# Pinning the first batch ahead of everything else in a linear-attention and Fourier-mixing kernel

## The chip, the cores and the metric

One core of one Trainium2 chip. The metric is device time in microseconds (us); a kernel's figure is the median of its runs, with the lowest and highest beside it. Engines are named as in the profile: PE is TensorE (matmuls), DVE is VectorE, ACT is ScalarE, POOL is GpSimd, SP is SyncE, which issues the input loads and the stores. "Landed" means that a transfer's data are in place, and "the cast" always means ScalarE's conversion of batch 2's first queries.

## The reference, cut to what matters

Batches are counted from 0 to 3. Each has 8 heads of 768 steps; the kernel takes heads in pairs, four to a batch.

```python
for t in range(S):                       # linear attention with decay, q, k, v: (4, 8, 768, 64)
    state = gamma * state + outer(k[:, :, t], v[:, :, t])
    y[:, :, t] = scale * (q[:, :, t] @ state)
x = y.transpose(0, 2, 1, 3).reshape(4, 768, 512)
mixed = real(fft(fft(x, axis=1), axis=2))            # mixing
u = x + mixed
un = (u - mean(u)) / sqrt(var(u) + 1e-6)
out = u + relu(un @ w_ch1) @ w_ch2                   # w_ch1 (512, 2048), w_ch2 (2048, 512)
```

## The kernel before, as far as the argument touches it

The loads of one head pair are three transfers, q, k and v of 384 KB each. `after` ties them to a weight transfer:

```python
def load_unit(b, i, after=None):
    def run():
        for name, src in srcs.items():
            t = inp.tile([P, 2, NCH, D], f32, tag="in32", name=f"{name}32")
            dma = nc.sync.dma_start(t, ...)                       # issued by SP
            if after is not None:
                tc.add_manual_dep(dma.ins, w_dma[after].ins.name, ...)   # "loads in turn"
# ... cut ...
def w1_unit(g):                                                   # w2_unit is alike; eight in all
    def run():
        w_dma.append(nc.gpsimd.dma_start(w116[...], moe_w_ch1[...]))     # issued by GpSimd, 512 KB
# ... cut ...
streams.append(([load_unit(1, i, 6) for i in range(4)], -0.1, 0.0))     # batch 1 waits for the 7th
```

Queries are cast to 16 bits on GpSimd for batches 0 and 1, on ScalarE for batches 2 and 3:

```python
def cast_unit(b, i):
    ...
        if b < NPE:                                    # NPE = 2
            ... nc.gpsimd.tensor_scalar(out=q16, in0=q32...)
        else:
            q16 = qzs[i % 2]
            for h2 in range(2):
                dst = q16[:, h2, :, D * h2:D * h2 + D]
                nc.scalar.copy(dst, q32[:, h2])        # "q16z<-q" on ACT
```

The first batch is a list of units (`un`) whose order is pinned on every engine. The rest is a set of streams: each has a start and an end on a common scale (1.0 is a batch), the units are sorted by it, and this gives each engine's order:

```python
un += [q0_unit(3), w1_unit(0), t0_unit(3, 0), te_unit(3, 0), filler(2)] + y(2)    # fourth pair
un += [yx_unit(2), ..., k0_unit(3), filler(2), ..., v0_unit(3), w1_unit(1), csn_unit(0), ...]
# ... cut ...
streams += [(majors, b, b + 1.0),                      # the two big matmuls, h (psh) and ch (psc)
            (mix_units(b, [3, 4, 5]), b + (0.12 if b == 0 else 0.02), b + 0.3)]
...
    ts = [0.04 + 0.57 * sum(n[:j]) / sum(n) for j in range(7)]    # attention of the next batch
    streams.append((mix_units(b + 1, [0, 1, 2]), b + ts[-1] + 0.09, b + ts[-1] + 0.24))
```

`filler(n)` is n matmuls on zeros that only keep TensorE busy.

Of the kernel before, what the change touches and what calls it, by code (L numbers as in the profile page):

```python
# [11 lines left out]
AF = mybir.ActivationFunctionType  # L12
ALU = mybir.AluOpType
# [5 lines left out]
P = 128  # L19
# [3 lines left out]
NCH = S // P  # L23
# [11 lines left out]
def kernel(  # L35
# [50 lines left out]
    sgn = const.tile([P, 1], f32, tag="sgn")  # L86


    tails = {}
    mark = [0]  # L90

    def pin(engines=None):
        ins = tc.nc.cur_bb.bb.instructions
        for n in range(mark[0], len(ins)):
            x = ins[n]
            e = str(x.engine)
            if engines is not None and not any(g in e for g in engines):
                continue
            if e in tails:
                tc.add_manual_dep(x, tails[e],  # L100
                                  mybir.DependencyInfo(mybir.DependencyClass.NoSync,
                                                       mybir.DependencyReason.DATA),
                                  reason="pinned order")
            tails[e] = x.name
        mark[0] = len(ins)


    ht16 = hp_.tile([P, NFB, 384], f16, tag="ht16")
# [3 lines left out]
    def filler(n):  # L112
        def run():
            for _ in range(n):
                nc.tensor.matmul(wps, wz[:, 0:P], wz, start=True, stop=True)  # L115
        return run
# [36 lines left out]
    icoln = const.tile([P, 5], f32, tag="icoln")  # L153
    hpi = const.tile([P, 1], f32, tag="hpi")

    nc.gpsimd.memset(wz, 0.0)  # L156
    nc.gpsimd.iota(icol_i[:, 0:3], pattern=[[P, 3]], base=0, channel_multiplier=1)
    nc.gpsimd.iota(icol_i[:, 3:5], pattern=[[P, 2]], base=1, channel_multiplier=1)
    nc.gpsimd.iota(icol_i[:, 5:6], pattern=[[0, 1]], base=127, channel_multiplier=-1)
    nc.gpsimd.iota(kf_i, pattern=[[1, KN]], base=0, channel_multiplier=0)  # L160
    filler(8)()
    for h in range(H):
        nc.vector.memset(lgrow[:, h:h + 1], float(lng[h]))
    nc.vector.memset(maskf, 1.0)
    nc.vector.memset(gkrow, 0.0)
    for h in range(H):
        nc.vector.memset(gkrow[D * (h % 2):D * (h % 2) + D, h // 2, 1:NCH - 1],
                         float(gam[h] ** P))
    nc.vector.tensor_copy(icol[:, 0:6], icol_i[:, 0:6])
    nc.vector.tensor_scalar(out=gexp[:, 0], in0=lgrow, scalar1=icol[:, 3:4],  # L170
                            scalar2=float(math.log(0.125)), op0=ALU.mult, op1=ALU.add)
    nc.vector.tensor_scalar(out=gexp[:, 1], in0=lgrow, scalar1=icol[:, 5:6], scalar2=None,
                            op0=ALU.mult)
    nc.scalar.activation(gexp, gexp, AF.Exp, bias=0.0, scale=1.0)
    make_identity(nc, ident16)
    nc.gpsimd.affine_select(out=maskf, in_=maskf, compare_op=ALU.is_ge, fill=0.0, base=0,
                            pattern=[[1, P]], channel_multiplier=-1)
# [4 lines left out]
    nc.vector.tensor_scalar(out=icoln[:, 3:5], in0=icol[:, 3:5], scalar1=float(1.0 / DM),  # L182
                            scalar2=None, op0=ALU.mult)
    nc.vector.tensor_copy(kf, kf_i)

    def gk_unit(hp):
        def run():
# [50 lines left out]

    def csn_unit(c):
        def run():  # L240
            nc.gpsimd.tensor_scalar(out=csn[:, c, :].rearrange("p (i t) -> p t i", t=2),
                                    in0=csp[:, :, c, 0:192], scalar1=1.0, scalar2=1.0,
                                    op0=ALU.mult, op1=ALU.mult)
        return run

    def td_dve(c):
        return trig_dve(3 + c, DM, 257, icol[:, 3 + c:4 + c], icoln[:, 3 + c:4 + c])
# [672 lines left out]
    def first_units():  # L920
        def a(i):
            un = [am_unit(i, 0), am_unit(i, 1)]
            return un

        def e(i, *hh):
            return [ae_unit(i, half, h2) for half, h2 in hh]

        def y(i):
            return [yi_unit(i, 0), yi_unit(i, 1)]

        def x(i):
            return [x0_unit(i, 0), x0_unit(i, 1)]

        std = ((0, 0), (0, 1), (1, 0), (1, 1))
        heads = ((0, 0), (1, 0), (0, 1), (1, 1))
        o = PAIR_ORDER
        un = [ts_dve(0), gk_unit(o[0]), gk_unit(o[1]), t_act(0, 0), t_act(0, 1), q0_unit(0),
              t0_unit(0, 0), filler(6), ts_dve(1), te_unit(0, 0), t_act(0, 2), ts_dve(2),
              t_act(1, 0), k0_unit(0), t0_unit(0, 1), filler(2), te_unit(0, 1), v0_unit(0),
              t_act(1, 1), t_act(1, 2)]  # L940
        un += a(0) + [filler(1), kv0_unit(0)] + e(0, *std) + [sc_unit(0)]
        un += [q0_unit(1), t0_unit(1, 0), t_act(2, 0), te_unit(1, 0), filler(2)] + y(0)
        un += [td_dve(0), t_act(2, 1), k0_unit(1), t0_unit(1, 1), te_unit(1, 1), yx_unit(0),
               filler(1)] + x(0) + [v0_unit(1), half_ids]
        un += a(1) + [kv0_unit(1)] + e(1, *std) + [sc_unit(1), t_act(2, 2), gk_unit(o[2])]
        un += [q0_unit(2), t0_unit(2, 0), te_unit(2, 0), filler(2)] + y(1)
        un += [td_dve(1), parity_consts, t_act(3, 0), t_act(3, 1), k0_unit(2), t0_unit(2, 1),
               te_unit(2, 1), yx_unit(1), filler(1)] + x(1) + [v0_unit(2)]
        un += a(2) + [kv0_unit(2)] + e(2, *std) + [sc_unit(2), t_act(3, 2), gk_unit(o[3])]
        un += [q0_unit(3), w1_unit(0), t0_unit(3, 0), te_unit(3, 0), filler(2)] + y(2)  # L950
        un += [yx_unit(2), fold_s(0, 0, 258, 0, 1), g0_unit(0, (0,)), k0_unit(3), filler(2),
               x0_unit(2, 0), t0_unit(3, 1), te_unit(3, 1), x0_unit(2, 1), filler(3),
               v0_unit(3), w1_unit(1), csn_unit(0), csn_unit(1), csn_unit(2)]
        un += [w1_unit(g) for g in range(2, 4)] + [w2_unit(g) for g in range(4)]
        un += a(3) + e(3, (0, 0), (1, 0)) + [kv0_unit(3), filler(3), sc_unit(3),
               t_act(4, 0), t_act(4, 1)]
        un += e(3, (0, 1), (1, 1))
        un += [yx_unit(3), yi_unit(3, 0), x0_unit(3, 0), filler(2), yi_unit(3, 1), x0_unit(3, 1),
               g0_unit(0, (1,))]
        un += [fold_s(0, 0, 130, 1, 2), fold_d(0, 0, (0,)), s1_unit(0, 0, 0), t_act(4, 2),  # L960
               fold_s(0, 130, 258, 1, 2), fold_d(0, 0, (1,)), fold_d(0, 1, (0,)), px_unit(0),
               xmean_unit(0), fold_d(0, 1, (1,)), s1_unit(0, 1, 0), s1_unit(0, 0, 1),
               s1_unit(0, 1, 1), px_unit(1), filler(1), g0_unit(0, (2,)), mean_unit(0)]
        un += [s2_unit(0, 0), s2_unit(0, 1), norm_unit(0, 0), gr_unit(0), gr_unit(1),
               px_unit(2), filler(4), unT_unit(0, 0), xmean_unit(1), mean_unit(1),
               norm_unit(0, 1), s2_unit(0, 2), xmean_unit(2), mean_unit(2), norm_unit(0, 2),
               gr_unit(2), gr_unit(3), edge_zeros, x_edges(1)]
        return un

    def mix_units(b, kbs):  # L970
        return [s2_unit(b, kb) for kb in kbs] + [unT_unit(b, kb) for kb in kbs]

    def emit(streams):
        ev = []
        for si, (units, t0, t1) in enumerate(streams):
            for i, u in enumerate(units):
                ev.append((t0 + (t1 - t0) * (i + 1.0) / len(units), si, i, u))
        ev.sort(key=lambda e: e[:3])
        for e in ev:
            e[3]()  # L980
            if e[0] < 1.0:
                pin(None if e[0] < 0.05 else ["Pool", "GpSimd"])

    pin()
    for u in first_units():
        u()
        pin()
    first.close()
    ps_pm = pool("ps_pm", 3, space=PSUM)
    late_consts()  # L990
    streams = []
    for b in range(B):
# [6 lines left out]
        else:  # L999
# [3 lines left out]
        majors += [h_unit(b, 1, fb) for fb in range(NFB)]  # L1003
        majors.append(rstd_unit(b, 1))
        majors += [ch_unit(b, 1, rb3, part) for rb3 in range(3) for part in range(4)]
        streams += [(majors, b, b + 1.0),
                    (mix_units(b, [3, 4, 5]), b + (0.12 if b == 0 else 0.02), b + 0.3)]
        if b + 1 < B:
            steps = attn_steps(b + 1)
            if b == 0:  # L1010
                streams.append(([load_unit(1, i, 6) for i in range(4)], -0.1, 0.0))
                streams.append(([qt_zeros], 0.1, 0.15))
                streams.append(([pad_unit], 0.9, 0.95))
                ts = (0.27, 0.31, 0.34, 0.42, 0.51, 0.60, 0.67, 0.74)
            else:
                streams.append(([load_unit(b + 1, i) for i in range(4)], b - 0.3, b + 0.15))
                n = [len(u) for u in steps]
                ts = [0.04 + 0.57 * sum(n[:j]) / sum(n) for j in range(7)]
                ts.insert(1, ts[1])
            streams.append((steps[0], b + ts[0], b + ts[1]))  # L1020
            streams += [(u, b + ts[j + 2], b + ts[j + 3]) for j, u in enumerate(steps[1:])]
            streams.append(([s1_unit(b + 1, 0, 1), s1_unit(b + 1, 1, 1)], b + ts[-1] + 0.04,
                            b + ts[-1] + 0.06))
            streams.append((mix_units(b + 1, [0, 1, 2]), b + ts[-1] + 0.09, b + ts[-1] + 0.24))
    emit(streams)


# [28 lines left out]
```

## Time and profile before

| kernel before | |
|---|---|
| median of 3 runs | 265.85 us (265.15 to 265.86) |
| span of the profiled run (a run of 264.69 us) | 263.0 us |
| PE, DVE, ACT, POOL busy | 92%, 70%, 44%, 29% |
| first h matmul, start | 39.48 us |
| loads of batch 1 released (seventh weight landed) | 42.75 us |
| the cast, start | 67.50 us |

Busy shares are averages over stages. The row of slices (a fortieth of the span each, busy share in tenths) shows the stages, and the chain, the waits and the timeline say what ended each wait. The lines that my prediction rested on are shown inside it. One row of the same page I passed over, the granted clock of TensorE in tenths of full speed:

```profile
PEclk9898899999999999999999999999999999999999
```

Three slices of the first five hold an 8: part of the time in them was granted at half speed (a clock of 0.50 for 3.41 us from 11.04 us and again from 24.69).

### The profile page before, as it was taken

How to read it: one execution, taken by the hardware profiler on the slowest of the kernel's cores; microseconds unless marked ns; L12 is line 12 of the kernel's file. 1: busy time of each engine (PE TensorE's matmuls, PEld its weight loads, DVE VectorE, ACT ScalarE, POOL GpSimd, SP SyncE). 2: the span in 40 equal slices, each digit the busy share in tenths (PEclk: the TensorE clock that was granted, in tenths of full speed). 3: DMA queues.
4: the chain of work that ended last, by engine and by line, in shares of the span. 5: the costliest groups of instructions: out<-in, count | busy, mean ns of one | idle time of the engine just before them, and what ended most of it. 6: DMA issues, size and time to landing. Idle time of an engine off the chain costs nothing.

```text
span 263.0 us, 5235 instructions
## 1 busy us (share of the span) xinstructions
PE 242.4 (92%) x2020; PEld 148.1 (56%) x2020; DVE 184.2 (70%) x446; ACT 115.9 (44%) x238; POOL 75.1 (29%) x132
## 2 busy tenths in 40 slices
PE   7497799979999998999999999999999999999993
PEld 2265468946675554766566545656567456445541
DVE  7889974959799876798885654997886737523421
ACT  3886469573574344564336422541245305402300
POOL 5776600398233042543201411410001303100000
PEclk9898899999999999999999999999999999999999
DMA  8999999999999899979974042264110231211012
GB/s 174 265 246 137 199 193 220 256 228 267 213 242 194 111 241 189 219 148 175 241 192 91 0 100 82 50 122 110 42 40 0 42 122 37 45 55 64 0 42 80
DMA packets 97432, 35.99 MB, mean 137 GB/s; under 512 B 88192, under 2 KB 94336, under 8 KB 97408
## 3 DMA queue, kind: packets, MB, share of 16 engines
q1 hardware_dynamic: 93184, 31.47, 57.5%
q0 software_dynamic: 4224, 4.19, 10.1%
q8 instruction: 16, 0.26, 0.4%
q14 instruction: 8, 0.07, 0.1%
HBM read 27.26 MB, written 6.29 MB: 128 GB/s over the span
## 4 chain that ended last, share of the span: by engine, by line
PE 56%; DVE 24%; ACT 8%; POOL 6%; issue 3%; DMA 1%; POOLq 0%; ACTq 0%; DVEq 0%
PE psc L866 23%; PE psh L829 19%; DVE bst L785 4%; POOL u L769 3%; PE ps L659 3%; DVE u L760 3%; POOL u L767 2%; PE wkA L540 2%; DVE ht L835 2%; PE wps L115 2%; DVE atm L411 2%; DMA qTz<-q16z 1%; DVE s L568 1%; DVE eo L628 1%; DVE atm L542 1%
## 5 line engine op out<-in xcount | busy, mean ns | idle before, releaser
L866 PE MATMUL psc<-w,ht 128*128 128x512 f16 x384 | 89.9, 379 | 0.6 <-DVE ht L835 0.6
L829 PE MATMUL psh<-unT,w 128*128 128x384 f16 x448 | 82.8, 326 | 2.6 <-DVE ht L835 1.6
L866 PEld LDWEIGHTS <-ht 128*128 128x128 f16 x384 | 36.5, 98 | 38.1 <-DVE ht L835 1.6
L829 PEld LDWEIGHTS <-w 128*128 128x128 f16 x448 | 42.8, 98 | 26.8 <-issue 3.4
L833 ACT ACTIVATE ht<-psh 128x384 f16<-128x384 f32 x56 | 27.2, 488 | 54.7 <-PE psh L829 54.7
L767 POOL TENSOR_TENSOR u<-u,x 128x256 f32<-128x256 f32 x21 | 13.4, 637 | 93.3 <-DVE u L760 90.9
L870 DVE SCALAR_TENSOR_TENSOR ob<-psc,stats,u 128x512 f32<-128x512 f32 x24 | 17.9, 746 | 28.1 <-PE psc L866 28.0
L835 DVE TENSOR_SCALAR ht<-psh 128x384 f16<-128x384 f32 x56 | 30.6, 547 | 8.3 <-PE psh L829 8.3
L542 DVE TENSOR_TENSOR atm<-wkA,maskp 128x512 f16<-128x512 f32 x36 | 23.9, 682 | 0.8 <-PE wkA L540 0.8
L787 ACT ACTIVATE un<-u,stats 128x512 f16<-128x512 f32 x21 | 15.2, 722 | 17.4 <-DVE stats L786 15.4
L323 POOL TENSOR_SCALAR kd<-k,gexp 128x384 f16<-128x384 f32 x24 | 13.9, 590 | 23.7 <-PE wkK L558 11.0
L785 DVE BATCH_NORM_STATS2 bst<-u 128x6 f32<-128x512 f32 x21 | 14.5, 693 | 7.7 <-POOL u L769 7.7
L601 ACT ACTIVATE x<-wkY,gexp 128x384 f16<-128x384 f32 x24 | 12.7, 582 | 14.4 <-PE wkY L593 14.4
L568 DVE SCALAR_TENSOR_TENSOR s<-s,gkrow,wkK 128x128 f16<-128x128 f16 x48 | 16.4, 341 | 1.3
L760 DVE SCALAR_TENSOR_TENSOR u<-pq,g,qn 128x257 f32<-128x257 f32 x24 | 11.5, 477 | 7.8 <-ACT qn L757 7.8
L115 PE MATMUL wps<-ht 128*128 128x512 f16 x40 | 14.2, 467 | 1.4 <-POOL ht L156 1.4
L769 POOL TENSOR_TENSOR u<-u,x 128x256 f32<-128x256 f32 x21 | 13.4, 636 | 2.5 <-DVE u L762 1.9
L540 PE MATMUL wkA<-qTz,kT 128*128 128x256 f16 x72 | 12.9, 272 | 0.2 <-ACT x L601 0.2
L321 ACT CAST q16z<-q 128x384 f16<-128x384 f32 x16 | 7.5, 512 | 12.6 <-DMA qTz<-q16z 8.0
L328 POOL TENSOR_SCALAR v<-v 128x768 f16<-128x768 f32 x12 | 10.0, 832 | 10.7 <-PE wkY L593 8.8
L846 PE MATMUL psh<-unT,w 128*128 128x128 f16 x192 | 11.7, 219 | 0.6 <-DVE ht L853 0.2
L757 ACT COPY qn<-pq 128x255 f32<-128x255 f32 x24 | 8.9, 371 | 6.9 <-PE pq L748 6.9
(141 smaller groups left out, 318.2 us busy)
## 6 DMA issues: line engine op xcount, KB each, us to landing
q<-in_q_dram SPq DMA_DIRECT2D x16, 384.0 KB, 5.4
k<-in_k_dram SPq DMA_DIRECT2D x16, 384.0 KB, 5.3
v<-in_v_dram SPq DMA_DIRECT2D x16, 384.0 KB, 6.3
out_dram<-ob SPq DMA_DIRECT2D x24, 256.0 KB, 2.2
w<-in_moe_w_ch_dram POOLq DMA_DIRECT2D x8, 512.0 KB, 9.0
unT<-un SPq DMA_TRANSPOSE x12, 2.4
qTz<-q16z SPq DMA_TRANSPOSE x8, 3.8
kT<-kd SPq DMA_TRANSPOSE x8, 2.8
```

Source lines behind the costliest of these rows:

```text
L115: nc.tensor.matmul(wps, wz[:, 0:P], wz, start=True, stop=True)
L540: nc.tensor.matmul(wk[:, c2], st["kT"][:, c, :], st["qT"][:, :, c, :], start=True, stop=True)
L542: nc.vector.tensor_tensor(out=st["atm"][:, 2 * part:2 * part + 2], in0=wk, in1=maskp[:, PAIR_ORDER[i]].unsqueeze(1).to_broadcast([P, 2, 2, ...
L568: nc.vector.scalar_tensor_tensor(out=s16[:, c], in0=s16[:, c - 1], scalar=gkrow[:, hp, 1:2], in1=wk[:, c - c0], op0=ALU.mult, op1=ALU.add)
L760: nc.vector.scalar_tensor_tensor(out=u[:, kb, 0:257], in0=psP, scalar=g0, in1=qn, op0=ALU.add, op1=op_lo)
L767: nc.gpsimd.tensor_tensor(out=u[:, kb, 0:256], in0=u[:, kb, 0:256], in1=x[:, kb, 0, 1:257], op=ALU.add)
L769: nc.gpsimd.tensor_tensor(out=u[:, kb, 256:512], in0=u[:, kb, 256:512], in1=x[:, kb, 1, 257:1:-1], op=ALU.add)
L785: nc.vector.bn_stats(bst, u[:, kb, :])
L829: nc.tensor.matmul(psh, w116[:, cb, fb * P:(fb + 1) * P], unT[:, cb, rt * 384:(rt + 1) * 384], start=(cb == 0), stop=(cb == 3))
L833: nc.scalar.activation(ht16[:, fb, :], psh, AF.Relu, bias=0.0, scale=-1.0)
L835: nc.vector.tensor_scalar(out=ht16[:, fb, :], in0=psh, scalar1=-1.0, scalar2=0.0, op0=ALU.mult, op1=ALU.max)
L866: nc.tensor.matmul(psc, ht16[:, fb, rb3 * P:(rb3 + 1) * P], w216[:, fb, :], start=(fb == 0), stop=(fb == NFB - 1))
```

## The change

Its intent is to start the first batch's stage of big matmuls earlier: load ScalarE's sine table at once, make all cosine and sine tables one pair ahead of the need, hold zero fills of later buffers back behind the first batch (`behind`), and give the transposes of rows (`unT`) more room, by splitting mixing from transposing in the streams. The diff, cut to its core:

```diff
+    def behind():                       # what is not of the first batch waits for its end, in order
+        for x in tc.nc.cur_bb.bb.instructions[mark[0]:]:
+            if str(x.engine) in base:
+                tc.add_manual_dep(x, base[str(x.engine)], ... reason="behind the first batch")
@@ start
-    nc.gpsimd.memset(wz, 0.0)           # now behind the four iotas
+    nc.scalar.activation(icol[:, 6:7], lgrow[:, 0:1], AF.Sin, bias=0.0, scale=1.0)
@@ csn_unit
-            nc.gpsimd.tensor_scalar(out=csn[:, c, :]..., in0=csp[:, :, c, 0:192], ...)
+            nc.scalar.activation(csn[:, c, :], rs[2 * c + 1][:, 0:384], AF.Sin, bias=hpi, ...)
@@ first_units  (td_dve, t_act, parity_consts one pair earlier; more fillers)
-        un += [q0_unit(3), w1_unit(0), t0_unit(3, 0), te_unit(3, 0), filler(2)] + y(2)
+        un += [q0_unit(3), t0_unit(3, 0), te_unit(3, 0), filler(3)] + y(2)
-        ... k0_unit(3), filler(2), ... v0_unit(3), w1_unit(1), csn_unit(0), csn_unit(1), csn_unit(2)]
+        ... k0_unit(3), w1_unit(0), filler(2), ... v0_unit(3)]
-        un += [w1_unit(g) for g in range(2, 4)] + [w2_unit(g) for g in range(4)]
+        un += [w1_unit(g) for g in range(1, 4)] + [w2_unit(g) for g in range(4)]
@@ streams
-        streams += [(majors, b, b + 1.0),
-                    (mix_units(b, [3, 4, 5]), b + (0.12 if b == 0 else 0.02), b + 0.3)]
+        t0 = b + (0.1 if b == 0 else 0.0)
+        s2s, unTs = mix_units(b, [3, 4, 5])
+        streams += [(majors, b, b + 1.0), (s2s, t0 + 0.02, t0 + 0.14),
+                    (unTs, t0 + 0.2, t0 + 0.28)]
-                ts = [0.04 + 0.57 * sum(n[:j]) / sum(n) for j in range(7)]
+                ts = [0.04 + 0.55 * sum(n[:j]) / sum(n) for j in range(7)]
-            streams.append((mix_units(b + 1, [0, 1, 2]), b + ts[-1] + 0.09, b + ts[-1] + 0.24))
+            streams.append((s2s, b + ts[-1] + 0.08, b + ts[-1] + 0.16))
+            streams.append((unTs, b + ts[-1] + 0.17, b + ts[-1] + 0.23))
```

More of the change, by code (lines that the diff above doesn't have):

```diff
@@ L86 @@
     sgn = const.tile([P, 1], f32, tag="sgn")
-    tails = {}
+    tails, base = {}, {}
     mark = [0]
@@ L105, in pin @@
         mark[0] = len(ins)
+    def behind():
+        for x in tc.nc.cur_bb.bb.instructions[mark[0]:]:
+            if str(x.engine) in base:
+                tc.add_manual_dep(x, base[str(x.engine)],
+                                  mybir.DependencyInfo(mybir.DependencyClass.NoSync,
+                                                       mybir.DependencyReason.DATA),
+                                  reason="behind the first batch")
     ht16 = hp_.tile([P, NFB, 384], f16, tag="ht16")
@@ L160 @@
     nc.gpsimd.iota(kf_i, pattern=[[1, KN]], base=0, channel_multiplier=0)
+    nc.gpsimd.memset(wz, 0.0)
     filler(8)()
@@ L164 @@
     nc.vector.memset(maskf, 1.0)
-    nc.vector.memset(gkrow, 0.0)
-    for h in range(H):
-        nc.vector.memset(gkrow[D * (h % 2):D * (h % 2) + D, h // 2, 1:NCH - 1],
-                         float(gam[h] ** P))
     nc.vector.tensor_copy(icol[:, 0:6], icol_i[:, 0:6])
@@ L184 @@
     nc.vector.tensor_copy(kf, kf_i)
+    nc.vector.memset(gkrow, 0.0)
+    for h in range(H):
+        nc.vector.memset(gkrow[D * (h % 2):D * (h % 2) + D, h // 2, 1:NCH - 1],
+                         float(gam[h] ** P))
     def gk_unit(hp):
@@ L240, in run @@
         def run():
-            nc.gpsimd.tensor_scalar(out=csn[:, c, :].rearrange("p (i t) -> p t i", t=2),
-                                    in0=csp[:, :, c, 0:192], scalar1=1.0, scalar2=1.0,
-                                    op0=ALU.mult, op1=ALU.mult)
+            nc.scalar.activation(csn[:, c, :], rs[2 * c + 1][:, 0:384], AF.Sin, bias=hpi,
+                                 scale=-float(2.0 * np.pi / S))
         return run
@@ L938, in first_units @@
               t0_unit(0, 0), filler(6), ts_dve(1), te_unit(0, 0), t_act(0, 2), ts_dve(2),
-              t_act(1, 0), k0_unit(0), t0_unit(0, 1), filler(2), te_unit(0, 1), v0_unit(0),
-              t_act(1, 1), t_act(1, 2)]
+              t_act(1, 0), t_act(1, 1), k0_unit(0), t0_unit(0, 1), filler(3), te_unit(0, 1),
+              v0_unit(0), t_act(1, 2), td_dve(0), t_act(2, 0)]
         un += a(0) + [filler(1), kv0_unit(0)] + e(0, *std) + [sc_unit(0)]
-        un += [q0_unit(1), t0_unit(1, 0), t_act(2, 0), te_unit(1, 0), filler(2)] + y(0)
@@ L943, in first_units @@
-        un += [td_dve(0), t_act(2, 1), k0_unit(1), t0_unit(1, 1), te_unit(1, 1), yx_unit(0),
-               filler(1)] + x(0) + [v0_unit(1), half_ids]
-        un += a(1) + [kv0_unit(1)] + e(1, *std) + [sc_unit(1), t_act(2, 2), gk_unit(o[2])]
+        un += [q0_unit(1), t0_unit(1, 0), t_act(2, 1), te_unit(1, 0), filler(3)] + y(0)
+        un += [td_dve(1), t_act(2, 2), t_act(3, 0), k0_unit(1), t0_unit(1, 1), te_unit(1, 1),
+               yx_unit(0), filler(2)] + x(0) + [v0_unit(1), half_ids]
@@ L946, in first_units @@
+        un += a(1) + [filler(1), kv0_unit(1)] + e(1, *std) + [sc_unit(1), t_act(3, 1)]
         un += [q0_unit(2), t0_unit(2, 0), te_unit(2, 0), filler(2)] + y(1)
-        un += [td_dve(1), parity_consts, t_act(3, 0), t_act(3, 1), k0_unit(2), t0_unit(2, 1),
-               te_unit(2, 1), yx_unit(1), filler(1)] + x(1) + [v0_unit(2)]
-        un += a(2) + [kv0_unit(2)] + e(2, *std) + [sc_unit(2), t_act(3, 2), gk_unit(o[3])]
-        un += [q0_unit(3), w1_unit(0), t0_unit(3, 0), te_unit(3, 0), filler(2)] + y(2)
@@ L951, in first_units @@
-        un += [yx_unit(2), fold_s(0, 0, 258, 0, 1), g0_unit(0, (0,)), k0_unit(3), filler(2),
-               x0_unit(2, 0), t0_unit(3, 1), te_unit(3, 1), x0_unit(2, 1), filler(3),
-               v0_unit(3), w1_unit(1), csn_unit(0), csn_unit(1), csn_unit(2)]
-        un += [w1_unit(g) for g in range(2, 4)] + [w2_unit(g) for g in range(4)]
-        un += a(3) + e(3, (0, 0), (1, 0)) + [kv0_unit(3), filler(3), sc_unit(3),
-               t_act(4, 0), t_act(4, 1)]
+        un += [parity_consts, t_act(3, 2), t_act(4, 0), gk_unit(o[2]), k0_unit(2),
+               t0_unit(2, 1), te_unit(2, 1), yx_unit(1), filler(3)] + x(1) + [v0_unit(2)]
@@ new lines, in first_units @@
+        un += a(2) + [filler(1), kv0_unit(2)] + e(2, *std) + [sc_unit(2), t_act(4, 1),
+                                                              gk_unit(o[3])]
+        un += [q0_unit(3), t0_unit(3, 0), te_unit(3, 0), filler(3)] + y(2)
+        un += [yx_unit(2), fold_s(0, 0, 258, 0, 1), g0_unit(0, (0,)), k0_unit(3), w1_unit(0),
+               filler(2), x0_unit(2, 0), t0_unit(3, 1), te_unit(3, 1), x0_unit(2, 1), filler(3),
+               v0_unit(3)]
+        un += [w1_unit(g) for g in range(1, 4)] + [w2_unit(g) for g in range(4)]
@@ L957, in first_units @@
+        un += a(3) + e(3, (0, 0), (1, 0)) + [kv0_unit(3), filler(4), sc_unit(3), t_act(4, 2),
+                                             csn_unit(0), csn_unit(1), csn_unit(2)]
         un += e(3, (0, 1), (1, 1))
         un += [yx_unit(3), yi_unit(3, 0), x0_unit(3, 0), filler(2), yi_unit(3, 1), x0_unit(3, 1),
-               g0_unit(0, (1,))]
-        un += [fold_s(0, 0, 130, 1, 2), fold_d(0, 0, (0,)), s1_unit(0, 0, 0), t_act(4, 2),
+               g0_unit(0, (1,)), filler(1)]
+        un += [fold_s(0, 0, 130, 1, 2), fold_d(0, 0, (0,)), s1_unit(0, 0, 0),
@@ L970, in mix_units @@
     def mix_units(b, kbs):
-        return [s2_unit(b, kb) for kb in kbs] + [unT_unit(b, kb) for kb in kbs]
+        return [s2_unit(b, kb) for kb in kbs], [unT_unit(b, kb) for kb in kbs]
     def emit(streams):
@@ L981, in emit @@
             if e[0] < 1.0:
+                behind()
                 pin(None if e[0] < 0.05 else ["Pool", "GpSimd"])
@@ L987 @@
         pin()
+    base.update(tails)
     first.close()
@@ L1021 @@
             streams += [(u, b + ts[j + 2], b + ts[j + 3]) for j, u in enumerate(steps[1:])]
-            streams.append(([s1_unit(b + 1, 0, 1), s1_unit(b + 1, 1, 1)], b + ts[-1] + 0.04,
-                            b + ts[-1] + 0.06))
-            streams.append((mix_units(b + 1, [0, 1, 2]), b + ts[-1] + 0.09, b + ts[-1] + 0.24))
+            streams.append(([s1_unit(b + 1, 0, 1), s1_unit(b + 1, 1, 1)], b + ts[-1] + 0.03,
+                            b + ts[-1] + 0.05))
+            s2s, unTs = mix_units(b + 1, [0, 1, 2])
+            streams.append((s2s, b + ts[-1] + 0.08, b + ts[-1] + 0.16))
+            streams.append((unTs, b + ts[-1] + 0.17, b + ts[-1] + 0.23))
     emit(streams)
```

## The prediction

> **What bounds the kernel now.** I read the page first, its slices above all. One digit is a fortieth of the span, 6.6 us.
>
> ```profile
> PE   7497799979999998999999999999999999999993
> DVE  7889974959799876798885654997886737523421
> DMA  8999999999999899979974042264110231211012
> ```
>
> From slice 8 on TensorE (PE) is at nine tenths or more. The stretches view says how full: up to 39.5 us, where the first h matmul starts, PE is busy 30.4 of 39.5 us, and of that 14.2 us are matmuls on zeros (40 of line 115) that only keep it busy; from 73.6 us on it is busy 179.9 of 189.4 us. So only the first batch can become much shorter. The third row warns: the DMA engines are at nine tenths or more from slice 2 to slice 13 (85 us) as well.
>
> Next the chain of work that ended last, in order of time, for the first batch:
>
> ```profile
> 6.36 0.54 ACT tmp L257
> 6.97 1.28 ACT L261
> 8.26 0.65 ACT csp L261
> ...
> 20.19 0.49 DVE tmp L232
> 21.58 1.85 DVE atm L411 x4
> 23.43 0.74 DVE s L435
> ```
>
> ScalarE (ACT) loads the sine table for 1.28 us in the middle of the chain, and VectorE (DVE) makes sine arguments (lines 228 to 232) and parity constants right ahead of the masks (atm) of the third head pair. Then the waits of the queue that issues the loads:
>
> ```profile
> SPq L129 <- DMA w<-in_moe_w_ch_dram: 26.2, 1, 26.2
> ```
>
> The twelve loads of batch 1 may start only when the seventh weight transfer has landed; this ends at 42.75 us. And of PE after 45 us:
>
> ```profile
> PE pst L816 <- ACT un L787: 2.3, 2, 1.4
> ```
>
> The transposes of rows (pst) cost PE 2.3 us, 1.4 at 56.2 us and 0.9 at 100.2 us by the timeline. Last, the timeline where the loads of batch 1 have run out:
>
> ```profile
> 62.38 0.39 SPq L129 DMA_DIRECT2D q<-in_q_dram  x1
> ...
> 67.50 0.51 ACT L321 CAST q16z<-q 128x384 f16<-128x384 f32 x1 [4.05 <-DMA q<-in_q_dram]
> 67.92 1.05 ACT L601 ACTIVATE x<-wkY,gexp 128x384 f16<-128x384 f32 x2
> ...
> 68.86 0.78 ACT L502 COPY qTz<-tq 64x768 f16<-64x768 f16 x1
> ...
> 69.67 0.96 DVE L502 COPY qTz<-tq 64x768 f16<-64x768 f16 x1 [0.79 <-ACT qTz L502]
> ```
>
> ACT stood idle 4.05 us until the first q of batch 2 landed. Behind it in ACT's order stand x and qTz, behind qTz DVE's half of qTz, ob and three atm, and the chain holds exactly these up to 73.2 us. This line decides my prediction.
>
> [...] weights (issued by GpSimd) and loads (issued by SP) together fill one DMA row. [...] The trace has a hole [...] (53 GB/s from 24 to 26 us, with two long DVE folds), but doesn't show its cause.
>
> **The change part by part.** The counts and orders are from comparing the two built programs.
>
> *Start.* The iotas come ahead of the 0.53 us zero fill, and six DVE memsets leave the front: two of 0.38 (qTz), two of q16z (0.42 together) and nine of gkrow that now come after kf. DVE's first cast (icol) came at 3.29, that of kf at 3.83, the sine arguments at 4.22. Now the first can start at about 1.35 and kf at 1.9; with 0.35 for kf and 0.84 for gkrow the arguments start at about 3.1, 1.1 us earlier. The table load moves to right after Exp (2.3 to 3.6 us, where ACT waited anyway). First kT evicted: 10.36 before; now about 8.5, since 1.1 + 1.28 are gained and a 0.65 us sine now stands ahead of it.
>
> *Tables ahead of the pairs.* Each set of three DVE instructions for cd/sd (about 1.2 us) moves ahead by one pair, into DVE's gaps (1.05 us before the first atm, about 1 before the second). The third pair's atm waits no more for 1.3 us of arguments. By adding durations in each engine's order I get its atm at 19.2 instead of 21.5.
>
> *Weights and csn.* The first weight transfer was issued at 19.10, ahead of the fourth k, which landed 3.15 us after its q where the other pairs need 1.6 to 1.8. Now it comes behind that k: k lands at about 20.0 instead of 21.5. csn leaves GpSimd (2.0 us) for ACT: three sines of about 0.65, in a gap before x of the last pair. Two more 0.38 us memsets leave DVE's chain (26.68 and 31.43). Fourth atm: about 25.0 instead of 28.1. After this the order is as before, so the first h matmul comes at about 36.2 instead of 39.5: **3.3 us gained by then**. Ten fillers more (0.22 to 0.4 each) stand where PE waits.
>
> *Batch 0 to 62 us.* Four qTz memsets (1.5 us) and two of q16z (0.4) now stand among the evictions of h0, where DVE is 4.64 of 5 us busy: up to 0.5 lost. The row transposes stand one to two groups of psc later: the 1.4 us wait goes. Lead at 62 us: about 4.
>
> *At 67.5 us.* What must flow through the DMA engines before that q is the same: 12 loads, 7 weights, 12 loads, one store, one load. What moves is only the holes. Before, the second weight was issued at 23.34 and the rate was 53 GB/s from 24 to 26. Now the first weight is issued at about 20.6 with the loads done at about 21.6; with the same 2.4 us from issue to flow there is a hole from 21.6 to 23.0. Seven weights of 524 KB at 196 GB/s (the rate from 26 to 40 us) take 18.7 us, and some of the eighth flows among them: the seventh lands at 42 to 42.6, against 42.7. So the load lands 0.1 to 0.8 us earlier, I say 0.4, and ACT, DVE and PE behind it come 0.4 earlier, not 4. **About 3.5 us of the lead are lost in one wait.**
>
> *After 73 us.* Fixed PE work. The 0.9 us wait for un at 100.2 goes, of which I count 0.7; the rest of the reordering (smaller spacing 0.55, s2 ahead of unT) I count 0.4, as the DVE waits for ht (1.4 us in three) may come or go.
>
> Sum: 265.85 - 0.4 - 0.7 - 0.4 = 264.35, so **264.3 us**.
>
> **Rivals.** *The lead survives.* If the q load came with the lead, 3.3 + 1.4 + 0.9 would give about 260.3, 2.1% faster. For it: the weights are issued 2.6 us earlier from the second on, and the 24 to 26 us hole (1.5 us of lost flow) may close. Against it: the row of nines and the 26.2 us wait. If the hole closes wholly, 1.4 us come through: about 263.3. *VectorE becomes the bound in h0.* The 1.9 us of memsets could stall h0's evictions beyond the lead: against it, PE has about 4 us to lose there before anything is later than now. *The weights come late for h0.* h0 needs the fourth weight by about 37.3; at 2.75 us each from 26.0 it lands at about 34.3, so no. *Reordering hurts later batches,* where PE has 5% of slack: up to +1, about 266.
>
> **Range and chances.** The wait on q gives 0.1 to 1.4, the later batches -0.5 to 1.8 of gain: 262.3 to 266.1 holds it 8 times in 10. Faster by over 2% needs under 260.6, that is nearly all of the lead: 0.05. Slower by over 2% needs a new stall of 5 us: 0.01.
>
> **What would show it.** Right: the table load at 2 to 4 us, the first h matmul at 35.5 to 37, no pst wait near 52 us, then an idle ACT of 6 us or more before the first q16z cast of line 330, which starts at 66.4 to 67.5, and PE idle of 2 to 4 us between 62 and 73. Wrong: the q16z cast at 64 or earlier (then the DMA engines had more room than I gave them), the first h matmul after 38 (then my sum of the first batch misses a wait), or PE idle after 73 that differs from now by over 2 us.

## The result, and the profile after

The changed kernel took **267.59 us (267.19 to 268.09, four runs)** against 265.86 (265.15 to 265.86, four runs). The ratio of the fast runs is 1.0073, 95% interval 1.0049 to 1.0096; a ratio is the mean time of one kernel's fast runs over that of the other's of the same rounds, so it is not quite the ratio of the medians. It is slower by a little, and outside my range. The two profiled runs took 264.69 and 268.09 us, 3.4 apart where the medians are 1.7 apart, so the traces overstate the difference.

The slices of the changed kernel's page:

```profile
PE   6898989799599998979998999999999999999993
DVE  7988867977399876788775753898686637623421
...
PEclk9999999999799999999999999999999999999999
DMA  8995999999999798979997032077110231312012
```

The start did what it should: the first h matmul starts at 36.01 us instead of 39.48. Two things are new. PE has a 5 in its eleventh slice, 66.6 to 73 us, and the DMA row has a 5 in its fourth, 20 to 26.6 us, where it had a 9.

The stores tell when the lead went. Each store waits for a sum on DVE (`ob`); the second at 64.99 before stands at 62.15 after, 2.84 us ahead, and the third at 70.67 before stands at 72.16, 1.49 us behind. ScalarE's and TensorE's timelines of the changed kernel in between (start, length, engine, line, operation; in brackets the idle time before and what ended it):

```profile
68.99 0.51 ACT L330 CAST q16z<-q 128x384 f16<-128x384 f32 x1 [8.37 <-DMA q<-in_q_dram]
69.41 1.06 ACT L610 ACTIVATE x<-wkY,gexp 128x384 f16<-128x384 f32 x2
```

```profile
66.54 0.38 PE L549 MATMUL wkA<-qTz,kT 128*128 128x256 f16 x2
70.04 0.59 PE L549 MATMUL wkA<-qTz,kT 128*128 128x256 f16 x2 [3.12 <-ACT x L610]
```

ScalarE stands idle 8.37 us for batch 2's queries. Behind the cast, in its order, is x, an output of batch 1's attention that has nothing to do with batch 2; the matmuls (`wkY`) that x is made from were through by about 64.3 us. TensorE waits 3.12 us for x, since the next scores (`wkA`) take their buffers from the same PSUM pool as `wkY`. This is the wait that I had predicted, but the cast comes 1.5 us later than before, not 0.4 earlier. Why, the queues say. First the wait of the loads of batch 1 in the changed kernel, then GpSimd's timeline there, then GpSimd's timeline before:

```profile
SPq L137 <- DMA w<-in_moe_w_ch_dram: 28.2, 1, 28.2
```

```profile
21.52 0.59 POOL L356 TENSOR_SCALAR kd<-k,gexp 128x384 f16<-128x384 f32 x1 [0.87 <-DMA k<-in_k_dram]
22.05 0.96 POOL L888 DMA_DIRECT2D w<-in_moe_w_ch_dram  x1
```

```profile
19.10 0.96 POOL L879 DMA_DIRECT2D w<-in_moe_w_ch_dram  x1
21.48 0.58 POOL L347 TENSOR_SCALAR kd<-k,gexp 128x384 f16<-128x384 f32 x1 [1.42 <-DMA k<-in_k_dram]
```

The fourth pair's k lands at 21.5 us in both kernels. Before, the first weight was issued while GpSimd waited for it, and its first data moved only at 20.8 us (between 18.5 and 20.7 only the queue of the loads moved packets), so it can't have held the loads up before that; now it is issued after that wait, at 22.05. The stretches of the changed kernel (window, length, PE busy with instructions, PE clock, DMA busy share, GB/s) show what the DMA engines did meanwhile:

```profile
20.00:21.00 1.00, 0.72 (x17) 1.00 0.89 143
21.00:22.00 1.00, 1.00 (x18) 1.00 0.12 19
22.00:23.00 1.00, 0.91 (x20) 1.00 0.02 4
23.00:24.00 1.00, 1.00 (x11) 1.00 0.16 29
24.00:25.00 1.00, 0.76 (x14) 1.00 0.67 77
```

They moved 19, 4 and 29 GB/s in the three microseconds in which, before, they moved 95, 204 and 203. The loads of batch 1 were released at 44.73 us instead of 42.75, and everything that flows behind them came later.

### The profile page after: what moved, and what is told of

It reads as the page before. It is cut to its first block, busy times and chain, and to the rows that moved or that the text cites. A ratio compares the mean times of both kernels' runs of the same rounds, so it can differ in the third digit from the quotient of the medians.

```text
span 266.4 us, 5255 instructions
## 1 busy us (share of the span) xinstructions
PE 244.5 (92%) x2030; PEld 147.9 (56%) x2030; DVE 183.8 (69%) x446; ACT 117.4 (44%) x242; POOL 74.2 (28%) x129
## 3 DMA queue, kind: packets, MB, share of 16 engines
HBM read 27.26 MB, written 6.29 MB: 126 GB/s over the span
## 4 chain that ended last, share of the span: by engine, by line
PE 45%; DVE 27%; ACT 8%; DMA 8%; POOL 5%; issue 3%; POOLq 0%; ACTq 0%; DVEq 0%
PE psc L875 21%; PE psh L838 12%; DMA q<-in_q_dram 4%; DVE bst L794 4%; POOL u L778 3%; DVE atm L551 3%; DVE atm L420 3%; DVE u L769 3%; ACT x L610 2%; PE ps L668 2%; DMA v<-in_v_dram 2%; POOL u L776 2%; DVE xab L627 2%; DVE eo L637 2%; DVE ob L879 2%
## 5 line engine op out<-in xcount | busy, mean ns | idle before, releaser
L838 PE MATMUL psh<-unT,w 128*128 128x384 f16 x448 | 84.4, 328 | 1.6 <-ACT ht L842 1.2
L551 DVE TENSOR_TENSOR atm<-wkA,maskp 128x512 f16<-128x512 f32 x36 | 23.8, 682 | 1.0 <-PE wkA L549 0.9
L123 PE MATMUL wps<-ht 128*128 128x512 f16 x50 | 16.4, 441 | 2.2 <-POOL ht L168 2.2
L549 PEld LDWEIGHTS <-kT 128*128 128x128 f16 x72 | 7.1, 99 | 9.9 <-issue 5.5
## 6 DMA issues: line engine op xcount, KB each, us to landing
w<-in_moe_w_ch_dram POOLq DMA_DIRECT2D x8, 512.0 KB, 12.3
```

Source lines behind the costliest of these rows:

```text
L549: nc.tensor.matmul(wk[:, c2], st["kT"][:, c, :], st["qT"][:, :, c, :], start=True, stop=True)
L551: nc.vector.tensor_tensor(out=st["atm"][:, 2 * part:2 * part + 2], in0=wk, in1=maskp[:, PAIR_ORDER[i]].unsqueeze(1).to_broadcast([P, 2, 2, ...
L838: nc.tensor.matmul(psh, w116[:, cb, fb * P:(fb + 1) * P], unT[:, cb, rt * 384:(rt + 1) * 384], start=(cb == 0), stop=(cb == 3))
```

## Experiments

All kernels below gave correct results. Runs e1 to e4 share one chip and the runs of before on it (266.09 us, 265.47 to 267.57); e5, e6, e7 and e9 another (265.66, 265.07 to 266.35); e8 and e10 to e12 ran later on that second chip (265.61, 265.07 to 266.35, the same runs of before and one more). The changed kernel itself was not timed in these rounds. The theory: ScalarE hands the lateness of a load on to TensorE through the cast, and the cast's time follows from when the first weight is issued. The main rivals: the reordering of later batches costs the time, or the transfers as a whole set the pace whatever the order.

### The place of the first weight and the mixing, each undone alone and together

e1 puts the first weight back ahead of the fourth k:

```diff
-        un += [q0_unit(3), t0_unit(3, 0), te_unit(3, 0), filler(3)] + y(2)
+        un += [q0_unit(3), w1_unit(0), t0_unit(3, 0), te_unit(3, 0), filler(3)] + y(2)
-        ... k0_unit(3), w1_unit(0), filler(2) ...
+        ... k0_unit(3), filler(2) ...
```

> The changed kernel with the first weight transfer back ahead of the fourth k (issued at about 19 to 20 us instead of 22.05). Theory A (the late weights push back the loads, and the first q cast of batch 2 holds ScalarE until its load lands): the seventh weight lands at about 42.7 instead of 44.7, that cast starts at about 67.5 instead of 69.0, and the time falls by 1.5 to about 266.1. Rival B (all of the loss is made by the reordering of batches 1 and 2, the late load is hidden): the cast comes earlier, the time stays at 267.6.

e2 does the reverse to the kernel before (`w1_unit(0)` behind `k0_unit(3)`):

> The kernel before with nothing changed but the first weight transfer issued behind the fourth k's cast. Theory A: it is issued at about 22, the seventh weight lands at about 44.7, the cast starts at about 69, and the time rises by about 1.5 to 267.4. Rival B: within 0.3 of 265.9. Rival C (the fourth k was late because of the weights): the fourth k lands at about 20 instead of 21.5; theory A says it stays at 21.5.

e3 is the change with the old places of mixing and transposes, and the old spacing, from batch 1 on:

```diff
+        if b == 0: ...                                  # as the change has it
+        else:
+            streams += [(majors, b, b + 1.0), (s2s + unTs, b + 0.02, b + 0.3)]
-                ts = [0.04 + 0.55 * ...
+                ts = [0.04 + 0.57 * ...
-            streams.append((s2s, ...+ 0.08, ...+ 0.16)); streams.append((unTs, ...+ 0.17, ...+ 0.23))
+            streams.append((s2s + unTs, b + ts[-1] + 0.09, b + ts[-1] + 0.24))
```

> The changed kernel with the old places of mixing and of row transposes from batch 1 on (and the old 0.57 spacing); batch 0 keeps the new ones. Theory A with a second loss of its own in the later batches: the cast stays at 69.0, the 1.9 us that the profile lost between 105 and 137 us go away, about 266.0. Rival D (the later loss follows from the late loads and not from the order): time stays at 267.6.

e4 is e1 and e3 together:

> Both at once: first weight early, old places from batch 1 on. If the two losses are separate and add up: cast at about 67.5, about 264.5 to 265.0, that is 0.9 to 1.4 under the kernel before. If the first batch's lead of about 3 us got through by itself: 262 or less. Theory A says it doesn't, as the cast still waits for its load.

| | median us | ratio to before (95%) |
|---|---|---|
| e1, first weight early | 266.90 | 1.0029 (1.0003 to 1.0055) |
| e2, before with it late | 266.87 | 1.0026 (1.0000 to 1.0053) |
| e3, old mixing | 266.38 | 1.0011 (0.9985 to 1.0038) |
| e4, both | 265.70 | 0.9985 (0.9957 to 1.0014) |

I had expected about 266.1, 267.4, 266.0 and 264.5 to 265.0 us: each moved the expected way, but by less (e1 ended 0.8, e3 0.4 and e4 0.7 us above its forecast, e2 0.5 below). The two parts add up. The weight's place costs 0.7 to 0.8 us, less than single runs are spread (1.3 to 1.6 us), though the casts in the traces move by 1.0 and 1.8 us with it: 266.38 - 265.70 with the old mixing, and 266.87 - 266.09 when it alone is moved in the kernel before (by the ratios of the changed kernel and e1, from different rounds, 1.2). The new mixing and spacing together cost 1.2 (266.90 - 265.70). With both undone the change is worth 0.4 us, an interval that holds zero: even then the lead of the first batch does not arrive. Four profiles say why, and three later repeats (e13 to e15) and e5 join them. Times in us:

| execution | first weight issued | batch 1's loads released | cast | third `ob` |
|---|---|---|---|---|
| e5 (below) | 17.80 | 40.65 | 65.55 | 68.71 |
| before | 19.10 | 42.75 | 67.50 | 70.67 |
| before, e14 | 19.13 | 42.52 | 67.48 | 70.64 |
| e1 | 20.37 | 43.09 | 68.02 | 71.18 |
| before, e13 | 20.46 | 43.20 | 68.30 | 71.47 |
| e4 | 20.50 | 42.74 | 67.85 | 71.02 |
| e3 | 21.71 | 44.46 | 68.89 | 72.06 |
| changed, e15 | 21.83 | 44.78 | 69.52 | 72.68 |
| before with it late, e2 | 21.86 | 44.84 | 69.33 | 72.50 |
| changed | 22.05 | 44.73 | 68.99 | 72.16 |

From the cast to the third `ob` it is 3.16 or 3.17 us in all ten, in old code and new, whatever lead there was 10 us earlier. The release follows 22.2 to 23.7 us after the first weight, the cast another 24.3 to 25.1 us later. The kernel before did it to itself in e13: there its first weight went out at 20.46 and its cast came at 68.30. In e1, e4 and e13 it went out 1.3 us later than in before because the work ahead of it on GpSimd, the fourth q's cast, waited 1.7 us for TensorE. GpSimd's cast of the fourth k starts at 21.2 to 21.5 us in all of them: the weight does not delay that load.

### The cast moved behind the work that it blocks

e6 is e4 with one constraint: ScalarE's two casts of batch 2's first queries come after x of batch 1's second pair. No transfer is moved by it.

```diff
+                    with ExitStack() as held:
+                        if (b, i) == (NPE, 0):
+                            held.enter_context(tc.issue_after(x_last[1].ins))
                         for h2 in range(2):
                             nc.scalar.copy(dst, q32[:, h2])
```

> The kernel of the e4 run (the change with the first weight issued early and the old mixing), with the two casts of the second batch's first pair of queries held in ScalarE's order behind the scaled keys x of the first batch's second pair. No load moves. Theory A: the lead of 2.9 us was lost because ScalarE, which runs in fixed order, stood at the casts for their load and the row work behind it came late; now TensorE no longer waits for x at 68 to 70 us, most of the lead of 2.9 us is kept through batch 1 and the time is 262.8 to 264.2 us (e4: 265.7). Theory B: the weights and the next batch's loads set the pace whatever the order is; TensorE meets the wait a few us later at the transposes of q or at the scores of batch 2, and the time stays at 265.2 to 266.2 us.

262.77 us (262.33 to 262.92, four runs), ratio 0.9890 (0.9872 to 0.9908), against 265.70 for e4 on the other chip. (The text calls x "scaled keys"; in the code it is the scaled output of the attention.) ScalarE's timeline of e6, x of the first pair, x of the second, the cast:

```profile
63.87 1.06 ACT L614 ACTIVATE x<-wkY,gexp 128x384 f16<-128x384 f32 x2 [3.55 <-PE wkY L606]
...
69.99 1.06 ACT L614 ACTIVATE x<-wkY,gexp 128x384 f16<-128x384 f32 x2 [0.45 <-PE wkY L606]
70.93 0.51 ACT L334 CAST q16z<-q 128x384 f16<-128x384 f32 x1
```

The cast is 3.1 us later than in e4 and waits for no load. x of the first pair, which in e4 ran at 68.27, runs at 63.87, as soon as its matmuls are done. TensorE's wait for x there (2.0 us in e4) is gone, and the third `ob` stands at 67.11 us instead of 71.02. So the loads as a whole did not set the pace; the order on ScalarE did. Of these 3.9 us the ratios keep 2.5: from the third `ob` to the end e6's trace takes 193.5 us, e4's 192.5. That ScalarE kept to this order the changed kernel's trace shows: it stood idle for 8.37 us up to the cast, and x behind the cast started at 69.41 us, some 5 us after its matmuls were through (64.3).

e9 is the changed kernel with this constraint alone:

> The changed kernel as it is, with only the two casts held behind x of the second pair. Seventh weight still lands at about 44.5 us and batch 2's first load at about 69 us. Theory A: the loss of 4.3 us between 65 and 71 us goes, stores at 72.2 us come at 67.8 to 68.5 us; the later loss of 1.4 to 1.9 us at 105 to 137 us may stay, so the time is 264.0 to 265.8 us (the change alone: 267.6 against 265.9). Theory B: the loads set the pace; 267 to 267.8 us.

263.96 us (263.27 to 265.69), ratio 0.9951 (0.9923 to 0.9979). The third `ob` stands at 67.34, even ahead of the 67.8 to 68.5 that theory A wanted.

e8 holds the casts in the kernel before:

> The kernel before, with only the two casts held behind x of the first batch's second pair. Its trace showed TensorE waiting just 0.2 us for x there. Theory A (the cast eats a lead, and the kernel before has none to eat): within 0.7 us of before, so that the gain of the held change (264.0 against 265.7) is the change's own lead set free. Rival: the casts cost the kernel before as much as the changed one, and holding them alone gives 262.8 to 264.3 us, so that the change itself is worth nothing even then.

264.17 us (263.44 to 266.47), ratio 0.9944 (0.9923 to 0.9964). This is a miss of my expectation (within 0.7 us of before): holding gains 1.4. So in this respect the rival was right. I had also misread the trace: the wait of 0.2 us for x stands at 172.5 us; at the cast before's TensorE did not wait for x at all. What holding frees is the row of work behind the cast, up to the third `ob`: with held casts this follows the second `ob` by 5.41 us (e8, and its repeat e16 below), in the three profiles of before by 5.68, 5.98 and 6.73. So the casts cost the kernel before 0.3 to 1.3 us, by the execution, which is most of the 1.4 at best. With its casts held, the change as it stands is worth nothing (263.96 against 264.17), and the change with the weight early and the old mixing 1.4 us (262.77 against 264.17). The traces show where it goes: at the third `ob` e9 (67.34) is 2.3 us ahead of e16 (69.62), but from there to the end e9 takes 194.2 us and e16 192.7, so that the later batches give 1.5 us of the lead back.

### The first weights put into the hole

e5 is e4 with two weights ahead of the fourth q on GpSimd, e7 the same with held casts:

```diff
-        un += [q0_unit(3), w1_unit(0), t0_unit(3, 0), te_unit(3, 0), filler(3)] + y(2)
+        un += [w1_unit(g) for g in range(2)] + [q0_unit(3), t0_unit(3, 0), te_unit(3, 0), ...] + y(2)
```

> The kernel of the e4 run, with the first two weights issued ahead of the fourth query's cast on GpSimd, at about 18 us, so that they fill the gap that the transfers show between 20 and 25 us. The casts stay where they are in ScalarE's order. Theory A (the in-order casts hand the load's time on, and the load hangs on when the weights are through): seventh weight at 41 to 41.6 us (e4: 42.7), casts at 66 to 66.6 us (e4: 67.9), about 1.3 us of the lead kept, 264.0 to 264.8 us. Theory B: the fourth key and value land later by as much as the weights take from them, the first batch's later pairs wait, and the time is 265.4 to 266.2 us.

> Both of the last edits on the kernel of the e4 run: the two first weights at about 18 us, and the casts held behind x of the second pair. Theory A: both reliefs act on the same wait, so the sum is not the sum of the two: with the casts held there is nothing left to gain from earlier weights unless TensorE meets the load itself; 262.3 to 263.8 us, and no slower than the better of the two alone. Theory B (loads set the pace whatever the order): as with the early weights alone, 264 to 264.8 us.

e5: 263.04 us (262.87 to 263.92), ratio 0.9907 (0.9890 to 0.9924), better than I had expected (264.0 to 264.8). GpSimd's and ScalarE's timelines of e5:

```profile
17.80 1.71 POOL L888 DMA_DIRECT2D w<-in_moe_w_ch_dram  x2
...
21.30 0.58 POOL L356 TENSOR_SCALAR kd<-k,gexp 128x384 f16<-128x384 f32 x1 [0.84 <-DMA k<-in_k_dram]
```

```profile
65.55 0.51 ACT L330 CAST q16z<-q 128x384 f16<-128x384 f32 x1 [4.07 <-DMA q<-in_q_dram]
```

Issued 2.7 us ahead of e4's, the weights bring the cast 2.3 us forward, and the fourth k is not late for it. e7: 262.42 us (261.36 to 263.68), ratio 0.9871 (0.9843 to 0.9899). As expected of two cures of one wait, the sum is little more than the better of the two.

### Which part of the reordering costs time

e10 and e11 put one part each back into e6, the spacing of 0.55 or the new places:

> The e6 kernel (262.8 us) with only the tighter spacing of the later batches' attention steps put back (0.55 for 0.57, and the first score pass 0.01 earlier), mixing and row transposes as in the kernel before. If the spacing is what costs the 0.9 to 1.2 us between 105 and 137 us (TensorE asks for the masked scores atm before VectorE has them, waits of 1.7 and 1.3 us), 263.5 to 264.2 us with those waits back; if not, 262.4 to 263.1 us.

> The e6 kernel with only the new places of the second score pass and the row transposes put back for the later batches, spacing 0.57 as in the kernel before. If these places are what costs the 0.9 to 1.2 us, 263.5 to 264.2 us and the waits for atm come back at 105 to 137 us; if the spacing does it, 262.4 to 263.1 us. One of this and the last run should hold the loss, or each a part.

e10: 263.41 us (262.40 to 263.75); e11: 263.75 us (262.68 to 264.27). By the medians each costs a part, 0.6 and 1.0, but e10 falls between its two forecasts, and the runs of each are spread over 1.4 and 1.6 us. TensorE's waits between 95 and 215 us (total, times, longest), of e11 first, then of e10:

```profile
PE wkA L553 <- DVE atm L555: 2.6, 2, 1.3
PE wkY L606 <- DVE atm L555: 1.7, 2, 1.2
PE pst L831 <- ACT un L802: 0.9, 1, 0.9
```

```profile
PE pst L831 <- ACT un L802: 0.9, 1, 0.9
PE psc L881 <- DVE ht L850: 0.5, 2, 0.3
```

The new places bring the waits for the masked scores `atm`, which the changed kernel has as well (1.3 and 1.7 us) and e6 and before have not. The spacing brings none. But the waits don't settle the cost: in return for them TensorE's waits of 1.5 us for `ht`, which e6 and before have, are gone, and from the third `ob` to the end e11's trace loses no more against before than e10's and e6's do (1.0 to 1.2 us each); those with both parts lose 1.3 (e1) to 1.9 (e9 and the changed kernel). e11's profiled run lost its time earlier, to a stretch of TensorE at half rate at 54 to 57 us (next section). So the loss of 1.2 us is shown for both parts together (e1 against e4), and the share of each is unresolved. The wait for `un`, which I wanted gone, is 0.9 us in all of them.

### Half rate on TensorE

The times of e7 fall into two groups: 261.36, 261.39 and 261.78 us at a mean granted clock of 1.00, and 263.06, 263.39 and 263.68 at 0.993. The traces show why the clock is under 1: one or two stretches of 3.4 us at half. In before's and the changed kernel's stretches:

```profile
21.29:24.70 3.41, 2.03 (x31) 1.00 0.96 154
24.70:28.10 3.40, 3.40 (x25) 0.50 1.03 149
```

```profile
65.95:69.36 3.41, 0.97 (x6) 1.00 1.28 254
69.36:72.76 3.40, 2.72 (x10) 0.50 1.21 246
```

In these two, as in e3 and e7, a half-rate stretch follows one in which PE was idle for some 1.4 to 2.4 us; but the same idle time at 51 to 53 us was followed by one in e1, e3 and e7 and not in the changed kernel, e4, e6 or e9. In the traces the half rate keeps to a fixed spacing: each half-rate stretch inside a span is 3.413 us long, and two in one trace start whole multiples of that apart (before: 11.04 and 24.69 us, four; e15: 54.59 and 71.65, five). With each trace divided into stretches of 3.413 us, counted from its own half-rate stretch, the idle time at 51 to 53 us falls into one of them in e1, e3 and e7 (PE busy 1.3 to 1.4 of 3.4 us) and is split over two in the changed kernel (2.2 and 2.5). So counted, in the 16 traces with half rate in their first 183 us (all but e6 and e9), every whole stretch up to there with PE busy less than 1.7 us was followed by half rate and none with more than 2.1; between the two both happened (2.03 us in before with half rate after it, 1.80 in e3 without).

It means two things. A half-rate stretch that the wait at the cast absorbed cost nothing: in e3 it fell at 54 to 57 us, in the changed kernel's profile at 69 to 73, and the third `ob` followed the cast by 3.17 us in both. A changed run with a clock of 1.00 took 267.59 us, no less than its fellows. But without the wait at the cast it counted: 1.9 us between the means of e7's two groups (261.5 and 263.4). And my lead of 3.3 us was read from a profile of before with two such stretches ahead of the first h matmul. This was still open, so before (e13, e14), the changed kernel (e15) and e8 (e16) were profiled again, on another chip:

> The kernel before, unchanged, for a second profile. If the lead is 1.2 us like for like, its first h starts at 37 us without any half-rate stretch ahead of it, at 38.1 with one at 11 to 15 us, and only with one at 24 to 28 us as well at 39.5; the casts of batch 2 stay at 67.5 us in all three cases and the stores follow 3.17 us later. If the lead is 3.3 us, the first h is at 39.3 to 39.6 us whatever the clock.

> The same kernel a third time, since the half-rate stretches fall differently in each execution: first h at 37.0, 38.1 or 39.5 us by the stretches ahead of it, casts at 67.5 us in each case.

> The changed kernel, unchanged, for a second profile: first h at 35.7 to 36.0 us without a half-rate stretch ahead of it, at 36.9 with one at 11 to 15 us; casts of batch 2 at 69.0 us and the stores at 72.1 to 72.2 us in either case.

> The kernel before with held casts, for a second profile (the first had two half-rate stretches and was its slowest run): with no or one stretch, no wait for x at the casts and the third stores' time at 69.0 to 70.2 us, 0.5 to 1.7 us ahead of before's 70.67; a span of 261.7 to 262.6 us as its other runs have.

With a half-rate stretch at 11 to 15 us alone, e14, before's first h matmul started at 39.15 us; with one at 22 to 26 as well, e13, at 39.24; e16, with only the later one, at 38.70. So I was wrong about its share: the stretch at 24 to 28 accounts for 0.3 us, not 1.4. The changed code has its first h at 36.9 with the early stretch (e5, e10, e12) and at 35.7 to 36.0 without. Like for like the lead is 39.15 - 36.9 = 2.3 us; without any stretch I have no profile of before. And e2, which is before but for the first weight's place, had its first h at 38.08 with the early stretch alone, 1.1 us ahead of e14. They part at two sums on DVE (`xab`), which take 2.47 us at 24.1 in e14 (2.46 in before's profile) and 1.37 at 23.8 in e2. In the changed kernel they run at 22.2 us, when `csn` is no longer on GpSimd beside them, and take 1.01. So about 1.1 of the 2.3 us hangs on these two instructions; why they take longer was not tested. The casts and third `ob` of e13 to e15 are in the table above: the casts did not stay at 67.5 and 69.0 in e13 and e15, as I had expected, but the third `ob` still followed by 3.16 or 3.17 us. In e16 the third `ob` stood at 69.62, in the range expected.

### A version that beats both

In e7 TensorE's first transposes of batch 1's queries wait for GpSimd, a wait that is new with the change. e12 puts them 1.5 us later in its order:

```diff
-                ts = (0.27, 0.31, 0.34, 0.42, 0.51, 0.60, 0.67, 0.74)
+                ts = (0.30, 0.33, 0.35, 0.42, 0.51, 0.60, 0.67, 0.74)
```

> The e7 kernel (262.4 us, 261.4 in runs without a half-rate stretch of TensorE's clock and 263.1 to 263.7 in those with one) with batch 2's first transposes of q and k some 1.5 us later in TensorE's order, behind four more second-stage matmuls and four row transposes. Its trace waited 1.5 and 0.6 us there for GpSimd's casts, and the half-rate stretch came right after. If those waits are on the path and call the half rate, they shrink below 0.8 us, the runs lose their slower half, and the time is 260.6 to 261.8 us. If the wait only moves to the row transposes or to what hangs on the later scores, 262 to 263.5 us.

(That text says "batch 2's first transposes"; it means the second batch in order, number 1.) **260.82 us (260.54 to 261.81, four runs), ratio 0.9826 (0.9804 to 0.9848)**, the fastest of all. TensorE's waits from 45 to 80 us, of e7 and of e12:

```profile
PE tq L509 <- POOL q16z L324: 1.5, 1, 1.5
PE tq L509 <- POOL kd L336: 0.6, 1, 0.6
```

```profile
PE tq L509 <- POOL kd L336: 0.6, 1, 0.6
PE tq L509 <- POOL q16z L324: 0.4, 1, 0.4
```

Of 2.1 us, 1.0 remain. Three of e12's runs have a clock of 1.00, and the profiled one has its half-rate stretch at 12 to 15 us. That this wait called the half rate is supported by this and not proved: e7's other runs have no trace.

## Why the prediction was wrong, point by point

- **Start and first h matmul: right.** Predicted 36.2 us, measured 36.01; the masks (`atm`) of the third and fourth pair came at 19.57 and 24.96 (predicted 19.2 and 25.0). That the lead came out at 3.5 us is partly luck: before's profile had two half-rate stretches ahead of its first h and the changed kernel's none. Like for like it is 2.3 (e14), and 1.2 against e2.
- **Batch 0 up to 62 us: partly wrong.** I had a lead of about 4 us there; the first two `ob` had 2.0 and 2.8. The wait of 1.4 us for the row transposes at 56 us did go, but TensorE got waits of 1.5 and 0.6 us for GpSimd's casts (`tq<-POOL`) in its place.
- **The lead dies at the cast: right.** ScalarE idled 8.37 us, TensorE waited 3.12 us between 62 and 73, as written. e6 and e9 show that the lead was lost there: moving the cast alone takes e4 from 0.9985 to 0.9890 of before's time and the changed kernel from 1.0073 to 0.9951, some 2.5 and 3.2 us of 266. Not all of that is the change's lead, since the same edit gains 1.4 in the kernel before (e8). One reading was wrong: I wrote that before's chain "holds exactly these", but x is not in it; ahead of qTz it has TensorE's transposes (`tq`, 68.16 to 68.84 us). Both x and `tq` were through at about 68.9 in that execution, so the cast was only just late enough to matter.
- **When the cast comes: the step that failed.** It rests on "k lands at about 20.0 instead of 21.5" and "the first weight is issued at about 20.6". I took the fourth k to be late because the weight was ahead of it; it was not. Its cast started at 21.2 to 21.5 in every run of the table, with the weight issued 3.5 us ahead of it in e5 as well as behind it. So the weight went out at 22.05. And even at the predicted 20.6 the table has the cast at 67.9 to 68.3, not the 67.1 that I made of it: the hole did not close as I had added it up. The seventh weight landed at 44.7, outside my "42 to 42.6", and the cast came 1.5 us later than before, outside my "66.4 to 67.5". The delay from issue to flow, 2.4 us, was about right: of the weight issued at 22.05 the first data moved at 23.8, and the rate reached 77 GB/s from 24 to 25 us. In the time this is +0.7 to 0.8 instead of -0.4.
- **After 73 us: wrong in sign.** I counted 0.7 and 0.4 of gain. The wait of 0.9 for `un` stayed, and the new places of mixing and transposes brought 3.0 us of waits for `atm` in the changed kernel, while some 1.5 us of waits for `ht` went. In medians the new places and the spacing together are about +1.2 (e1 against e4) instead of -1.1. The rival that I had listed, "Reordering hurts later batches, up to +1", was true.
- **The sum.** -0.4 (e4 against before), +0.7 for the weight and +1.2 for the mixing make +1.5; the change measured +1.7. Not settled are the shares of e10 and e11, why the fourth k lands late, why half rate followed some stretches with PE busy 1.7 to 2.1 of 3.4 us and not others, and the lead without any half-rate stretch in before.

## What to carry to other kernels

An engine that works in the order it is given and is half idle can still carry a wait from a load to work that has nothing to do with it: ScalarE, busy for 44% of the changed kernel's span, stood idle 8.37 us at the cast, and x behind it started some 5 us after its input was ready. If a batch ahead is cast on such an engine, try the cast behind the work of the batch at hand; here every gain ahead of it ended there until that was done. Before an issue is moved behind a load, find out from the trace whether the load is late because of it; and read the clock row before a lead is taken from one profile.

## What the traces show of the weights

The median from issue to landing of a weight, of which 512 KB are written, was 9.0 us before and 12.3 us after. No loads flowed beside the weights from 26 to 40 us: they queued behind one another, at 196 GB/s of what is written in before (197 after), which makes 2.7 us each, as an estimate from that rate. They are converted on the way: the page of the profile has 27.26 MB read from HBM, which is the 48 loads of 384 KB and eight weights of 1 MB.
